# A recurrent attention with an expert layer behind it: y made transposed by products into 32-partition groups, the bonus added on TensorE, four more transposes by DMA

## The chip, the cores and the metric

The kernel runs on one core of a Trainium2 chip. The metric is the device time of one execution in microseconds. Before the change three runs took 178.69 to 178.74 us, with a median of 178.7 us.

## The reference

```python
def _attn_ref(r, k, v, w, u):            # each (4, 8, 768, 48): batch, heads, steps, width
    for t in range(S):
        cur = einsum('bhd,bhe->bhde', u[None] * kt, vt)
        y[:, :, t] = einsum('bhd,bhde->bhe', rt, state + cur)
        state = wt[:, :, :, None] * state + einsum('bhd,bhe->bhde', kt, vt)

def _moe_ref(x, w_in, w_out):            # x (3072, 384), w_in (384, 2048), w_out (2048, 384)
    h = x @ w_in
    g = np.maximum(0.01 * h, h)
    return g @ w_out
...
x = attn_out.transpose(0, 2, 1, 3).reshape(B * S, H * D)
```

Each of 4 x 8 heads keeps a 48 x 48 state that decays per row by w. The output of a step is r times the state, plus the bonus: the sum over d of r k u, times v. The eight heads of a step side by side make a row of 384 numbers, and all 3072 rows go through two dense layers with a leaky rectifier between.

## The kernel before, in words

The steps are cut into 24 chunks of 128. Within a chunk the recurrence is a masked product of r and k, both scaled by running products of w, times v; the state carries what came before. The first four chunks are worked as two pairs (`pair`), whose steps lie interleaved on the partitions; the other 20 are worked one by one (`single`), some of them two at a time in one score step (`run`, `MERGED`). Two of the 20 are the first of their batch and have no state to read.

A single chunk n goes so. SyncE loads w, k, r and v (L708). ScalarE takes the logarithm of w (L718), TensorE sums it over the steps (L724, and totals in L727), VectorE makes the inclusive sum `ci` (L736), ScalarE the two exponentials (L750, L754), VectorE scales r and k into `rk` (L407). r and k are then turned so that the width lies on the partitions (`rkT`): for chunks in `RK_DMA` by one transposing DMA on SyncE's queue (L771), for the others by eight transposes on TensorE (L418) and two copies out of PSUM (L423 on VectorE, L425 on ScalarE). TensorE makes the scores (L864, 48 rows, even and odd heads in the two halves of the array's rows), VectorE masks them into `m` (L795). TensorE adds k times v to the state (L805, L820), and makes y: four products of `rkT` with the decayed state `sb` (L831, 96 columns each) and eight of `m` with `vb`, the bf16 copy of v (L836, 48 columns each). So y has the steps on the partitions.

The bonus runs beside it: GpSimd multiplies k by u and the result by r (L437, L441), VectorE sums it per head (L445), GpSimd multiplies v by that sum into `vs` (L449). For single chunks VectorE adds `vs` to y while it copies y out of PSUM (`add_bonus`, L482). For pairs TensorE adds it by a product with `spread` (L676), and y is copied out after (L686, L688).

The dense layers need y turned, with 384 numbers on 3 x 128 partitions (`xT`). `to_xt` does that by three transposes on TensorE (L468) and a copy out of PSUM (L473 on VectorE, L475 on ScalarE). For the six chunks of `Y_DMA` one transposing DMA does it (L849).

The dense layers take blocks of one or two chunks: up-projections of `xT` with `w_in_b` (L1030), the rectifier on ScalarE (L1045), down-projections (L1060). The last seven blocks use a scheme of seven products for two chunks (`seven`; sums on VectorE in L941, products in L960, output sums in L981).

Everything is issued in an order written out by hand: `ORDER` lists the steps, `FORCE` names the engine of those that have a choice. A small planner inside (`Plan.order`) walks that list, gives out buffers and counts expected times; they only decide how many products of zeros (`warm`, L1099) are put into TensorE's gaps in the first 24 us. [...]

Of the kernel before, what the change touches and what calls it, by code (L numbers as in the profile page):

```python
# [7 lines left out]
F32 = mybir.dt.float32  # L8
BF16 = mybir.dt.bfloat16
AF = mybir.ActivationFunctionType  # L10
ALU = mybir.AluOpType
# [11 lines left out]
class Plan:  # L23
# [75 lines left out]
TY = (0.95, 24, 0.7, -0.6)  # L99
ORDER = [1122, 0, 1, 2, 3, 4, 5, 6, 7, 11, 14, 20, 12, 18, 15, 17, 16, 13, 19, 21, 8, 22, 25, 26, 27, 23, 36,  # L100
# [67 lines left out]
def kernel(  # L168
# [22 lines left out]
    NQ = FF // 512  # L191
    JQ = NJ // NQ

    RK_DMA = {6, 11, 12, 14, 15, 16, 17, 18, 19, 20, 21, 22, 23}
    Y_DMA = {16, 17, 20, 21, 22, 23}
    MERGED = {6, 10, 12, 14, 16, 18, 20}
    LEAD = 4
# [62 lines left out]
    with tc.manual_schedule():  # L260
# [199 lines left out]
        def to_xt(P0, y, yp, s_ye, n):  # L460
            col_of = columns(n)

            def yT():
                return yp.t[:].bitcast(BF16).rearrange("p (g t) -> p g t", t=128)
# [669 lines left out]
```

## Time and profile before

| | us |
|---|---|
| median of three runs | 178.7 |
| profiled execution, its own time | 178.69 |
| its span | 177.0 |
| TensorE busy, products | 170.4 |
| TensorE busy, weight loads | 139.9 |
| VectorE busy | 143.5 |
| ScalarE busy | 114.0 |
| GpSimd busy | 107.3 |

The span runs from the first to the last instruction of the program in the trace. A group line has the code line, the engine, what it writes and reads, the shape and the count; then the busy time, the mean length of one and the idle time of the engine before it with what ended it. In a timeline the first figure is the start, the second the length until the last of the group has ended. Products on TensorE are pipelined and their ends are modelled: the next one starts long before the one before it ends, so lengths overlap, and the cost of a product is read from the difference of two starts.

### The profile page before, as it was taken

The numbers are of one execution on the slowest core, as the hardware profiler recorded it, in microseconds if no ns is written. First come the engines' busy times: TensorE is split into PE (matmuls) and PEld (weight loads), VectorE is DVE, ScalarE is ACT, GpSimd is POOL, SyncE is SP. The second block draws the span as 40 slices with busy tenths as digits, with TensorE's granted clock in tenths as the row PEclk, the third lists the DMA queues.
The fourth block names the chain that finished last, engine by engine and source line by source line (L and its number), as shares of the span: only waits on it lengthen the run. The fifth ranks groups of instructions, "written<-read, shape, count | busy, mean of one in ns | idle before, by whom it ended". The sixth has DMA issues, their size and how long they took to land.

```text
span 177.0 us, 5530 instructions
## 1 busy us (share of the span) xinstructions
PE 170.4 (96%) x2155; PEld 139.9 (79%) x2158; DVE 143.5 (81%) x299; ACT 114.0 (64%) x263; POOL 107.3 (61%) x143
## 2 busy tenths in 40 slices
PE   7999999999999999999999999999999998999993
PEld 2566779867768877777779899899899997799992
DVE  7498935267599899889879999999999999956662
ACT  5676769734677794796379964676769950178500
POOL 5989946486749859879599093391693959100000
PEclk9999999999999999999999999999999999999999
DMA  5999999999999999999999999996999897432104
GB/s 138 261 271 340 350 300 195 351 231 199 201 206 195 191 199 227 163 201 179 198 206 195 197 208 209 163 222 124 210 194 196 188 226 78 118 101 80 44 26 157
DMA packets 115885, 34.25 MB, mean 194 GB/s; under 512 B 108305, under 2 KB 115090, under 8 KB 115858
## 3 DMA queue, kind: packets, MB, share of 16 engines
q1 hardware_dynamic: 115856, 33.89, 93.1%
q8 instruction: 17, 0.28, 0.7%
q14 instruction: 10, 0.08, 0.2%
q10 hardware_dynamic: 2, 0.00, 0.0%
HBM read 25.17 MB, written 4.72 MB: 169 GB/s over the span
## 4 chain that ended last, share of the span: by engine, by line
PE 69%; DVE 15%; ACT 5%; issue 4%; DMA 3%; POOL 2%; DVEq 0%; SPq 0%; ACTq 0%
PE ps L1030 30%; PE ps L1060 13%; PE ps L960 10%; DVE rk L407 3%; DMA rkT<-rk 3%; PE ps L864 3%; DVE in L941 2%; PE ps L418 2%; ACT g L425 2%; PE ps L724 1%; PE ps L836 1%; DVE ci L736 1%; PE ps L518 1%; DVE dg L445 1%; ACT ps L750 1%
## 5 line engine op out<-in xcount | busy, mean ns | idle before, releaser
L1030 PE MATMUL ps<-xT,w_in_b 128*128 128x256 bf16 (+1 forms) x672 | 70.8, 258 | 0.3 <-DVE rk L407 0.2
L1045 ACT ACTIVATE g<-ps 128x512 bf16<-128x512 f32 x96 | 54.4, 598 | 18.1 <-PE ps L1030 16.0
L1030 PEld LDWEIGHTS <-w_in_b 128*128 128x128 bf16 x672 | 56.9, 98 | 7.8 <-issue 0.6
L437 POOL TENSOR_TENSOR ru<-in,ub 128x384 f32<-128x384 f32 x24 | 24.3, 1017 | 13.1 <-DMA in<-in_k_dram 7.0
L1060 PE MATMUL ps<-w_out_b,g 128*128 128x384 bf16 x160 | 31.4, 326 | 0.0
L407 DVE TENSOR_TENSOR rk<-in,ps 128x384 bf16<-128x384 f32 x48 | 24.8, 547 | 6.1 <-ACT ps L754 2.3
L782 POOL TENSOR_TENSOR sb<-s,a 128x384 bf16<-128x384 f32 x18 | 15.6, 875 | 16.6 <-ACT a L745 8.1
L795 DVE TENSOR_TENSOR m<-ps,maskb 128x512 bf16<-128x512 f32 x40 | 25.1, 682 | 0.3 <-PE ps L864 0.2
L441 POOL TENSOR_TENSOR ru<-ru,in 128x384 f32<-128x384 f32 x24 | 23.8, 1000 | 2.1 <-DMA in<-in_r_dram 1.1
L1060 PEld LDWEIGHTS <-g 128*128 128x128 bf16 x160 | 14.1, 97 | 6.8
L449 POOL TENSOR_TENSOR vs<-in,dg 128x384 f32<-128x384 f32 x20 | 17.4, 874 | 3.0 <-DMA in<-in_v_dram 2.1
L960 PEld LDWEIGHTS <-g 128*128 128x128 bf16 x224 | 18.3, 98 | 0.2
L976 ACT COPY o<-ps 128x192 f32<-128x192 f32 x18 | 5.8, 320 | 17.5 <-PE ps L960 15.5
L960 PEld LDWEIGHTS <-in 128*128 128x128 bf16 x168 | 13.6, 98 | 1.9 <-DVE in L941 1.4
L445 DVE TENSOR_REDUCE dg<-ru 128x8 f32<-128x384 f32 x24 | 12.9, 545 | 1.9 <-POOL ru L441 1.7
L457 POOL CAST vb<-in 128x384 bf16<-128x384 f32 x24 | 12.7, 534 | 2.2 <-DMA in<-in_v_dram 2.2
L981 DVE TENSOR_TENSOR o<-ps,o 128x192 f32<-128x192 f32 x35 | 11.6, 351 | 1.9 <-ACT o L976 1.1
L482 DVE TENSOR_TENSOR y<-ps,vs 128x384 bf16<-128x384 f32 x20 | 10.9, 553 | 2.4 <-PE ps L836 2.3
L754 ACT ACTIVATE ps<-ci 128x384 f32<-128x384 f32 x20 | 9.8, 493 | 4.7 <-DVE ci L736 4.1
L718 ACT ACTIVATE lw<-in 128x384 bf16<-128x384 f32 x20 | 9.9, 521 | 4.1 <-DMA in<-in_w_dram 4.1
L736 DVE TENSOR_TENSOR ci<-ps,lw 128x384 f32<-128x384 f32 x20 | 10.9, 551 | 1.8 <-PE ps L724 1.1
L960 PE MATMUL ps<-in,in 128*128 128x192 bf16 x112 | 11.4, 247 | 0.5 <-DVE in L941 0.5
(105 smaller groups left out, 258.8 us busy)
## 6 DMA issues: line engine op xcount, KB each, us to landing
out_dram<-o SPq DMA_DIRECT2D x23, 192.0 KB, 2.8
in<-in_w_dram SPq DMA_DIRECT2D x20, 192.0 KB, 4.7
in<-in_k_dram SPq DMA_DIRECT2D x20, 192.0 KB, 4.2
in<-in_r_dram SPq DMA_DIRECT2D x20, 192.0 KB, 4.2
in<-in_v_dram SPq DMA_DIRECT2D x20, 192.0 KB, 4.1
in<-in_moe_w_out_dram SPq DMA_DIRECT2D x4, 768.0 KB, 6.9
in<-in_moe_w_in_dram SPq DMA_DIRECT2D x2, 768.0 KB, 9.7
in<-in_moe_w_in_dram SPq DMA_DIRECT2D x4, 384.0 KB, 8.1
```

Source lines behind the costliest of these rows:

```text
L407: (nc.gpsimd if e == "POOL" else nc.vector).tensor_tensor(out=o, in0=x, in1=i, op=ALU.mult)
L437: lambda e: nc.gpsimd.tensor_tensor(out=ru.t[:], in0=kv(), in1=ubv, op=ALU.mult),
L441: lambda e: nc.gpsimd.tensor_tensor(out=ru.t[:], in0=ru.t[:], in1=rv(), op=ALU.mult),
L445: lambda e: nc.vector.tensor_reduce(out=dg.t[:], in_=ru.t[:], axis=AX.X, op=ALU.add),
L449: lambda e: nc.gpsimd.tensor_tensor(out=vs.t[:], in0=vv(), in1=dg.t[:].unsqueeze(2).to_broadcast([128, H, D]), op=ALU.mult),
L457: {"POOL": 0.56}, lambda e: nc.gpsimd.tensor_copy(out=vb.t[:], in_=vv()),
L782: lambda e: nc.gpsimd.tensor_tensor(out=sb.t[:].rearrange("p g a d -> p (g a) d"), in0=s_in.t[:].rearrange("p g a d -> p (g a) d"), in1=a_ ...
L795: lambda e, par=par: nc.vector.tensor_tensor(out=m.t[:, par, :, :], in0=sc[par].t[:].rearrange("p (g t) -> p g t", g=NP), in1=maskb[:].uns ...
L960: nc.tensor.matmul(o(), lhsT=x()[:, i, :], rhs=y()[:, i, :], start=fresh, stop=(stop and i == ii[-1]), skip_group_check=True)
L1030: nc.tensor.matmul(hp.t[:, a * N : (a + 1) * N], lhsT=w_in_b[:, t, (j + a) * 128 : (j + a + 1) * 128], rhs=xb.t[:, t, 0:N], start=(a == 0 ...
L1045: lambda e, hp=hp, g=g, j=j, J=J, N=N: nc.scalar.activation(out=g.t[:, j : j + J, 0:N], in_=hp.t[:, 0 : J * N].rearrange("p (a n) -> p a n ...
L1060: nc.tensor.matmul(op.t[:, 0:DM], lhsT=g.t[:, j, off : off + 128], rhs=w_out_b[:, j, :], start=(j == 0), stop=(j == NJ - 1))
```

## The change

y is made turned from the beginning. The operands of its products change places: `vb` and `sb` become the stationary side, cut into pieces of 32 columns, and `m` and `rkT` the moving side, 128 steps wide. Each product so fills 32 partitions of PSUM and 128 columns; `cell` gives the place. Twelve pieces of 32 make the 384 numbers. The eight heads of 48 do not divide by 32, so `vb` gets a layout in which each head has 80 places, the last 32 zero, and the middle piece of each pair of heads is added up from two products. Per single chunk there are 12 products with the state and 16 with v, instead of four and eight.

The bonus is added by TensorE into the same bank: `vs` (now bf16) is the stationary side, the identity matrix the moving one, three products per chunk (for pairs `spread`). Then one copy, on VectorE or ScalarE, takes the bank, now f32, into `xT`. The transposes of y (L468), the addition on VectorE (L482), the copies of the pairs' y (L686, L688) and the DMAs of y (L849) are gone. `RK_DMA` gains chunks 8, 9, 10 and 13. `vb` is cleared once at the start. `ORDER` and `FORCE` are written anew.

```diff
-TY = (0.95, 24, 0.7, -0.6)
...
-    RK_DMA = {6, 11, 12, 14, 15, 16, 17, 18, 19, 20, 21, 22, 23}
-    Y_DMA = {16, 17, 20, 21, 22, 23}
+    RK_DMA = {6, 8, 9, 10, 11, 12, 13, 14, 15, 16, 17, 18, 19, 20, 21, 22, 23}
...
-    make("vb", 6, [128, H, D], BF16)
+    make("vb", 6, [128, NP, 2, 80], BF16)
...
-    make("vs", 4, [128, H, D], F32)
+    make("vs", 4, [128, H, D], BF16)
...
+        for t in pools["vb"]:
+            nc.vector.memset(t[:, :, :, D:80], 0.0)
...
+        def cell(bank, g, i):
+            t, q = divmod(3 * g + i, 4)
+            return bank.t[32 * q : 32 * q + 32, t * 128 : (t + 1) * 128]
+
+        def xt_copy(P0, yp, n, deps):
             col_of = columns(n)
...
             def xcopy(e):
+                src = yp.t[:, 0:DM].rearrange("p (t c) -> p t c", t=KT)
                 if e == "DVE":
-                    nc.vector.tensor_copy(out=col_of(), in_=yT()[:, 0:KT, :])
+                    nc.vector.tensor_copy(out=col_of(), in_=src)
                 else:
-                    nc.scalar.copy(out=col_of(), in_=yT()[:, 0:KT, :])
...
+            return step({"ACT": 0.5, "DVE": 0.55}, xcopy, P0 + 1, deps=deps, reads=[yp], takes=[place[n][0]])
...
+        def turn_y(n, P0, first, m, vb, rkT, sb, vs, deps, s_vs):
+            yp = Buf("ps", "yy")
+
+            def intra(e):
+                for i in range(0 if first else 3):
+                    for p in range(NP):
+                        nc.tensor.matmul(
+                            cell(yp, p, i), lhsT=sb.t[:, p, :, :].rearrange("p a d -> p (a d)")[:, 32 * i : 32 * i + 32],
+                            rhs=rkT.t[:, p, :], start=(i == 0), stop=False, skip_group_check=True)
+                for i, x in ((0, 0), (1, 1), (1, 2), (2, 3)):
+                    for p in range(NP):
+                        nc.tensor.matmul(
+                            cell(yp, p, i), lhsT=vb.t[:, p, :, :].rearrange("p a d -> p (a d)")[:, 32 * x : 32 * x + 32],
+                            rhs=m.t[:, x // 2, p, :], start=(first and x == 0), stop=False, skip_group_check=True)
+
+            s_y = step({"PE": 0.28 if first else 0.44}, intra, P0 + 1, deps=deps,
+                reads=[m, vb, rkT] + ([] if first else [sb]), takes=[yp])
+
+            def add_vs(e):
+                for t in range(KT):
                     nc.tensor.matmul(
+                        yp.t[:, t * 128 : (t + 1) * 128],
+                        lhsT=vs.t[:].rearrange("p h d -> p (h d)")[:, t * 128 : (t + 1) * 128], rhs=ident[:],
+                        start=False, stop=True, skip_group_check=True)
+
+            s_yb = step({"PE": 0.18}, add_vs, P0 + 1, deps=[s_y, s_vs], reads=[yp, vs])
+            xt_steps[n] = [xt_copy(P0, yp, n, [s_yb])]
...
-            s_ye = add_bonus(P0, y, yp, vs, s_y, s_vs)
-            if n not in Y_DMA:
-                xt_steps[n] = [to_xt(P0, y, yp, s_ye, n)]
-            else:
...
+            turn_y(n, P0, first, m, vb, rkT, sb, vs, [*s_m, *s_T, s_vb, s_sb], s_vs)
```

The pairs' products change in the same way: their products with v use 64 rows and 32 columns of the array, two row halves for two output banks, 64 of them per pair instead of 32, and 12 products with the state instead of four.

More of the change, by code (lines that the diff above doesn't have):

```diff
@@ L673, in add_vs @@
                 for j in range(2):
-                    for x in range(2):
-                        q = slice(64 * x, 64 * x + 64)
-                        nc.tensor.matmul(
-                            yps[x].t[:, 0:DM], lhsT=spread[q, j, :], rhs=vss[j].t[q, :, :].rearrange("p h d -> p (h d)"),
-                            start=False, stop=(j == 1), skip_group_check=True)
-            s_yb = step({"PE": 0.4}, add_vs, P0 + 1, deps=[s_y, *s_vss], reads=[*yps, *vss])
-            for x in range(2):
-                y = Buf("y")
-                def evac_y(e, y=y, x=x):
-                    if e == "DVE":
-                        nc.vector.tensor_copy(out=y.t[:], in_=heads(yps[x].t))
-                    else:
-                        nc.scalar.copy(out=y.t[:], in_=heads(yps[x].t))
-                s_ye = step(
-                    {"ACT": 0.48, "DVE": 0.55}, evac_y, P0 + 1, deps=[s_yb] + [s_yi] * x, reads=[yps[x]], takes=[y])
-                xt_steps[n + x] = [to_xt(P0, y, yps[x], s_ye, n + x)]
-                rows[n + x] = out[b * S + x * L : b * S + (x + 1) * L, :]
+                    for t in range(KT):
+                        for x in range(2):
+                            q = slice(64 * x, 64 * x + 64)
+                            nc.tensor.matmul(
+                                yps[x].t[:, t * 128 : (t + 1) * 128],
+                                lhsT=vss[j].t[q, :, :].rearrange("p h d -> p (h d)")[:, t * 128 : (t + 1) * 128],
+                                rhs=spread[q, j, :], start=False, stop=(j == 1), skip_group_check=True)
@@ L805, in sums @@
                         nc.tensor.matmul(
[L806 removed]
+                            pp.t[:, p * 2 * D : (p + 1) * 2 * D].rearrange("p (a d) -> p a d", a=2),
                             lhsT=rk.t[:, 1, 2 * p : 2 * p + 2, :].rearrange("p h d -> p (h d)"),
[L808 removed]
+                            rhs=vb.t[:, p, :, 0:D],
                             start=True, stop=True, skip_group_check=True)
```

102 lines of the change are left out of this document (38 added, 64 removed), and 104 rows, old and new, of the table ORDER.

## The prediction

> **What bounds the kernel now.** I read the page first, then the stretches, then TensorE's own timeline.
>
> ```profile
> span 177.0 us, 5530 instructions
> PE 170.4 (96%) x2155; PEld 139.9 (79%) x2158; DVE 143.5 (81%) x299; ACT 114.0 (64%) x263; POOL 107.3 (61%) x143
> ...
> PEclk9999999999999999999999999999999999999999
> ...
> PE 69%; DVE 15%; ACT 5%; issue 4%; DMA 3%; POOL 2%; DVEq 0%; SPq 0%; ACTq 0%
> ```
>
> TensorE is busy 96% of the span at a full clock and holds 69% of the chain that ended last. Its busy time is modelled, so the starts have to show whether it is really full.
>
> ```profile
> 54.13 0.81 PE L1060 MATMUL ps<-w_out_b,g 128*128 128x384 bf16 x4
> 54.78 0.83 PE L1030 MATMUL ps<-xT,w_in_b 128*128 128x128 bf16 x12
> 55.45 0.33 PE L831 MATMUL ps<-sb,rkT 128*128 128x96 bf16 x4
> 55.62 0.36 PE L836 MATMUL ps<-vb,m 128*128 128x48 bf16 x8
> 55.82 0.83 PE L1030 MATMUL ps<-xT,w_in_b 128*128 128x128 bf16 x12
> ...
> 56.86 0.32 PE L724 MATMUL ps<-lw,trev 128*128 128x384 bf16 x1
> 57.02 0.24 PE L727 MATMUL ps<-ones,lw 128*128 128x1 bf16 x4
> ```
>
> Columns: start, length, then the group. Differences of starts give the rates: 0.65 us for 4 products of 384 columns, 0.67/12 = 0.0558 for one of 128 columns, 0.17 for the four state products, 0.20 for eight of 48 columns (0.0255 each, more than 48 columns would need). No gap stands between groups, so from here on each added column is paid for. The gaps that do exist:
>
> ```profile
> 48.35 0.81 PE L1060 MATMUL ps<-w_out_b,g 128*128 128x384 bf16 x4
> 49.20 0.49 PE L836 MATMUL ps<-vb,m 128*128 128x48 bf16 x8
> 49.81 0.40 PE L418 MATMUL ps<-ident,rk 128*128 128x128 bf16 x4
> ```
>
> ```profile
> 149.01 0.83 PE L960 MATMUL ps<-w_out_b,in 128*128 128x192 bf16 x8
> 150.38 0.84 PE L960 MATMUL ps<-in,in 128*128 128x192 bf16 x8 [0.53 <-DVE in L941]
> 151.61 0.83 PE L960 MATMUL ps<-w_out_b,in 128*128 128x192 bf16 x8 [0.40 <-DVE in L941]
> 152.38 0.40 PE L864 MATMUL ps<-rkT 48*128 48x128 bf16 x8
> ```
>
> At 48 to 50 us, 0.85 + 0.61 pass where 0.65 + 0.20 are work: 0.6 lost. At 149 to 152, 1.37 and 1.23 pass for eight products each, which take 0.66 elsewhere (118.40, in the chain further down): 1.3 lost to late sums of VectorE. That is 1.9 us in all, the most that a relief of VectorE can return after the start.
>
> ```profile
> 127.00:152.00 25.00, 24.04 (x316) 21.86 (x315) 24.79 (x46) 14.36 (x39) 19.00 (x23) 1.00 0.99 179
> ```
>
> Columns: stretch, length, busy time of TensorE, its weight loads, VectorE, ScalarE, GpSimd, then clock, DMA share, GB/s. In the stretch of the second loss VectorE is full (24.79 of 25.00).
>
> **The change, part by part.** TensorE first, chunks 4 to 23. Removed: 18 sets of state and value products at 0.17 + 0.20 and two sets of 0.20, 7.06 us; the transposes of y of 14 chunks, 42 products of 128 columns at 0.0558, 2.34; the transposes of r and k of four chunks, 32 products, 1.79.
>
> Added: 12 products per chunk with state (18) and 16 for each of 20, 536 in all, each 128 columns wide into 32 partitions, four partition groups side by side. Do four run at once? The trace has no such form; the nearest is the pairs' score product, 48 rows into 64 partitions, two row halves by two column halves:
>
> ```profile
> 11.08 0.64 PE L632 MATMUL ps<-g 48*64 48x128 bf16 x32 [0.17 <-ACT g L425]
> ```
>
> ```profile
> L632 PE MATMUL ps<-g x64: 213/216/241, 11.1 to 19.0; 48*64 48x128 bf16 x64
> ```
>
> One of these lasts 216 ns (the middle figure), so 32 starts lie within 0.42: 0.0137 each, a quarter of 0.0558. Four parts of the array did run at once, with weight loads between them. I take 0.0140 per product, 536 x 0.0140 = 7.50. The bounds are 0.0137 and, if nothing runs at once, 0.0558 (+22 us). The bonus adds 60 products of 128 columns, 3.35.
>
> Each change of the array's division has a price too. The scores of the chunks use two row halves:
>
> ```profile
> 35.60 0.33 PE L724 MATMUL ps<-lw,trev 128*128 128x384 bf16 x1
> 35.85 0.40 PE L864 MATMUL ps<-rkT 48*128 48x128 bf16 x8
> 36.18 2.77 PE L1060 MATMUL ps<-w_out_b,g 128*128 128x384 bf16 x16
> ```
>
> ```profile
> 52.24 0.62 PE L864 MATMUL ps<-rkT 48*128 48x128 bf16 x16
> 52.80 0.82 PE L1060 MATMUL ps<-w_out_b,g 128*128 128x384 bf16 x4
> ```
>
> Eight take 0.33 to the next start, sixteen 0.56: 0.23 per eight, so 0.10 is the way out. The product of 384 columns before them holds 0.25 where 0.16 is usual (56.86 to 57.02): 0.09 for the way in. That is 0.20 for a visit. In the changed order the 20 chunks' new products stand in 15 runs, each with whole-array products on both sides; the scores keep 13 visits. Whether a division by columns costs what one by rows costs, no row shows; bounds are 0 and 0.20, and I take 0.20, since the score row is the only one: 3.0 us.
>
> Sum: 7.50 + 3.35 + 3.0 - 7.06 - 2.34 - 1.79 = +2.7 us of TensorE.
>
> VectorE and ScalarE:
>
> ```profile
> L482 DVE TENSOR_TENSOR y<-ps,vs 128x384 bf16<-128x384 f32 x20 | 10.9, 553 | 2.4 <-PE ps L836 2.3
> ...
> L473 DVE COPY xT<-ps 128x384 bf16<-128x384 bf16 x9 | 3.1, 355 | 1.5 <-PE ps L468 1.5
> ...
> L1071 DVE COPY o<-ps 128x384 f32<-128x384 f32 x5 | 2.8, 550 | 0.0
> ```
>
> ```profile
> L475 ACT COPY xT<-ps 128x384 bf16<-128x384 bf16 x9 | 4.1, 481 | 3.1 <-PE ps L468 3.0
> ...
> L1073 ACT COPY o<-ps 128x384 f32<-128x384 f32 x5 | 2.4, 477 | 0.2 <-PE ps L1060 0.2
> ```
>
> VectorE loses 20 additions (11.1) and nine copies (3.2) and gets five copies of the new, wider form, priced as the other f32 copy, 0.55 (2.75); ScalarE has 19 of them at 0.48 instead of nine at 0.48. That is 11.5 us less on VectorE, before other copies that the new order hands to it; the exact size does not enter the sum, only whether it is late. Off TensorE's path this is worth nothing; where it was late it can return 0 to 1.9. I take 1.3, the loss at 149 to 152, because the additions of the chunks then in work leave VectorE; the earlier 0.6 stays.
>
> Queues: six transposing DMAs of y go, four of r and k come.
>
> ```profile
> 93.88 1.24 SPq L771 DMA_TRANSPOSE rkT<-rk  x1
> ...
> 117.50 2.48 SPq L849 DMA_TRANSPOSE xT<-y  x2
> ```
>
> Both kinds hold SyncE's queue for 1.24, so loads behind them get 2.5 us more room in all; the four new ones (chunks 8, 9, 10 and 13) stand early, among the loads of later chunks, which queue behind them while they wait for r and k. I cost it at nothing: the whole-array products of other chunks run meanwhile. Without that cover, one landing of 5.12 us (below) would be bare. GpSimd's narrower product and padded cast stay on an engine that is 61% busy, at nothing, bounded by a tenth of a microsecond per chunk either way. A new wait: the bonus product waits on TensorE for GpSimd's product, and everything on TensorE queues behind it.
>
> The start:
>
> ```profile
> 2.59 0.70 DVE rk L270 x5
> ...
> 3.56 0.56 DVE o L384
> ...
> 4.84 0.50 PE ps L395
> ...
> 18.53 0.74 ACT w_in_b L344
> 19.32 2.14 PE ps L1030 x18
> ...
> 108.18 5.12 DMA rkT<-rk
> ...
> 118.40 0.66 PE ps L960 x8
> ```
>
> In this chain of waits five clearings take 0.70; six more, of the padding of v, come ahead of the first addition: +0.85. Later the chain passes a weight cast that need not move. On the other hand only 6 up-projections, not 18, now precede the second pair's products (256 columns each, so twice 0.0558: 12 x 0.11 = 1.3 more afterwards). Against that, the pairs' y is no longer copied, transposed and copied. Bounds 0 and +2.2; I take +0.4.
>
> Sum: 2.7 - 1.3 + 0.4 = +1.8. The profiled execution took 178.69 us (span 177.0 and 1.7 around it), the median of the runs is 178.7, so 178.69 + 1.8 = 180.5 us.
>
> **Rivals.** First, the weight loads do not hide. In the new form all tiles lie in the same rows, and every product is preceded by a load; in the score row half the neighbours differ in rows. If each product then costs what the 48-column ones cost, 0.0255, 536 x 0.0115 = +6.2: 186.7. Against it: in the whole array, loads in the same rows already pass under products (128 columns each 0.0558). [...]
>
> Second, the other side: entering a division by columns costs nothing, because all rows stay in use. Then the 3.0 falls away at the 15 visits: 177.5, faster. It decides once a visit costs less than 0.08 (1.8/15 below 0.20). For it: the price is shown for row halves alone. Against it: the output products after the scores need nothing from them and still start late, so the price belongs to the change of division.
>
> Third, the stalls do not go but move: TensorE waits for the bonus or for a landing of r and k. The 1.3 is not gained and 20 waits of 0.1 come: 183.8. For it: the 5.12 landing in the chain; against it: GpSimd is idle 39% of the span.
>
> Fourth, the terms cancel: a visit at half the price and a little more relief, within 0.2% (0.36 us, about what a measurement of this kernel can tell from no change).
>
> **How the numbers follow.** Forecast 0.43, its own range 179.1 to 182.2; first rival 0.10; second 0.27; third 0.13; fourth 0.07. Faster: the second and a tail of the forecast, 0.28; same 0.08; slower 0.64. The range reaches to the second rival with all 1.9 returned, 176.9, and between the third and the first, 185.0.
>
> **What would show it.** Starts of the new products 0.014 apart in runs of 28 confirm the rate; 0.025 or more brings the first rival. The whole-array group ahead of them 0.1 late and the one behind 0.1 late confirm the visit. Gaps of TensorE gone at 149 to 152 confirm the relief; gaps ahead of the bonus products speak for the third rival. The first long run of up-projections after the second pair should begin within 1 us of 23.3; much earlier or later, and the start was mis-sized. A total of TensorE starts that falls instead of rising makes the forecast wrong.

## The result, and the profile after

The changed kernel takes 183.05 us (median of 4 runs, 182.72 to 183.49), the kernel before 178.72 us beside it: a ratio of 1.0243, 95% interval 1.0216 to 1.0271. It is slower by 4.3 us, where 1.8 was forecast. The profiled execution took 183.34 us, its span is 181.6 us (177.0 before).

From the page of the changed kernel:

```profile
span 181.6 us, 6248 instructions
...
PE 175.3 (97%) x2549; PEld 141.3 (78%) x2552; DVE 137.3 (76%) x284; ACT 114.3 (63%) x259; POOL 106.1 (58%) x142
...
q8 instruction: 20, 0.33, 0.8%
...
PE 88%; DVE 5%; DMA 3%; SPq 1%; issue 1%; DVEq 0%
```

TensorE's share of the chain rose from 69% to 88%. The third line is a queue that the prediction never looked at. Its 20 packets (0.33 MB, 16,384 bytes each in the trace) stand beside the 2549 products and 2552 loads of the line above, 255 to a packet; in the kernel before 17 packets stand beside 2155 and 2158, 254 to a packet. By this count I take it for the queue that brings TensorE's instructions.

First the part after the start. TensorE's timeline of the changed kernel (start, length, group):

```profile
45.13 1.46 PE L1048 MATMUL ps<-w_out_b,g 128*128 128x384 bf16 x8
46.52 0.41 PE L689 MATMUL ps<-m,vb 128*32 128x128 bf16 x16
46.86 1.48 PE L1048 MATMUL ps<-w_out_b,g 128*128 128x384 bf16 x8
```

```profile
59.41 0.35 PE L684 MATMUL ps<-rkT,sb 128*32 128x128 bf16 x12
59.58 0.40 PE L689 MATMUL ps<-m,vb 128*32 128x128 bf16 x16
59.81 0.34 PE L684 MATMUL ps<-rkT,sb 128*32 128x128 bf16 x12
59.97 0.40 PE L689 MATMUL ps<-m,vb 128*32 128x128 bf16 x16
60.30 0.82 PE L1048 MATMUL ps<-w_out_b,g 128*128 128x384 bf16 x4
```

Twelve products of 32 columns pass in 0.17 us and sixteen in 0.23: 0.014 each, a quarter of the 0.0558 of a product of 128 columns in the whole array, so four do run at once, and their loads, 95 and 97 ns each on average, are hidden. The visit is there too: eight products of 384 columns before the group take 1.39 where 8 x 0.162 = 1.30 is usual (0.09 in), and sixteen new ones hold 0.34 to the next start instead of 0.22 (0.12 out): 0.21 in all.

```profile
119.89 0.83 PE L948 MATMUL ps<-w_out_b,in 128*128 128x192 bf16 x8
120.56 0.82 PE L948 MATMUL ps<-in,in 128*128 128x192 bf16 x8
121.22 0.82 PE L948 MATMUL ps<-in,g 128*128 128x192 bf16 x8
121.88 0.82 PE L1018 MATMUL ps<-xT,w_in_b 128*128 128x256 bf16 x6
```

The products that waited for VectorE's late sums now follow each other every 0.66. After 28 us the starts show two waits in the whole span, 0.6 us together, at 44.87 and 139.72. The kernel before has 2.5 us by the same count: the prediction's two places come to 1.7, and it passed over 0.3 at 44.31, 0.2 at 113.35 and 0.2 at 145.98.

Now the start, where the rest went:

```profile
13.89 0.64 PE L619 MATMUL ps<-g 48*64 48x128 bf16 x32
...
20.44 0.92 PE L1087 MATMUL ps<-zeros 128*128 128x512 bf16 x5
21.30 0.64 PE L619 MATMUL ps<-g 48*64 48x128 bf16 x32
21.87 0.83 PE L1018 MATMUL ps<-xT,w_in_b 128*128 128x256 bf16 x6
22.53 1.19 PE L1087 MATMUL ps<-zeros 128*128 128x512 bf16 x7
...
24.37 0.91 PE L645 MATMUL ps<-m,vb 64*32 64x128 bf16 x64
...
26.45 0.71 PE L1018 MATMUL ps<-xT,w_in_b 128*128 128x256 bf16 x5
```

The same in the kernel before:

```profile
18.59 0.64 PE L632 MATMUL ps<-g 48*64 48x128 bf16 x32
19.32 2.14 PE L1030 MATMUL ps<-xT,w_in_b 128*128 128x256 bf16 x18
...
21.74 0.56 PE L657 MATMUL ps<-vb,m 64*128 64x48 bf16 x32
...
23.25 2.14 PE L1030 MATMUL ps<-xT,w_in_b 128*128 128x256 bf16 x18
```

The first pair's scores stand at 13.89 (11.08 before), the second's at 21.30 (18.59), its products of y at 24.37 (21.74), and the gapless work begins at 26.45 (23.25) with only 6 up-projections done, not 18. So 2.8 us are lost ahead of the first scores and come back nowhere. Products of zeros stand where work stood. For these kernels I count, in the first 30 us, the time that dummy products hold TensorE (start of each to the next start). Beside it stands how far TensorE is behind the kernel before at 30 us: the products that both have in common and that are still to be done, each at its usual spacing:

```
kernel                                dummy   behind at 30 us (us)
before                                  8.5    0
changed                                12.3    3.8
x1  clearings later                    11.2    3.6
x3  start in the old order              8.7    3.5
x5  few dummy products                  5.5    5.2
x9  all in the old order               10.2    2.4
x10 x9, clearings later                 9.6    1.9
x13 x10, dummy products halved          9.9    2.7
x16 x10, pairs in the old form          8.9   -0.5
x17 before, pairs in the new form       9.5    0.8
x11 before, new order of the start     13.4    5.0
x12 changed, with extra visits         12.4    4.1
```

The start costs 3.8 us: 29 up-projections of 256 columns (3.2), three of 128 (0.2) and four products of 384 columns (0.65) are left that the kernel before has done by then, against one product of 384 columns done ahead of it (0.16). What the pairs save by their new form is already in it. One profiled execution places such milestones only to within some half a microsecond: x12 below has the changed kernel's start unchanged, and its first scores stand at 13.36.

### The profile page after: what moved, and what is told of

Same layout as the page of the kernel before. It is cut to its first block, busy times and chain, and to the rows that moved or that the text cites. A ratio compares the mean times of both kernels' runs of the same rounds, so it can differ in the third digit from the quotient of the medians.

```text
span 181.6 us, 6248 instructions
## 1 busy us (share of the span) xinstructions
PE 175.3 (97%) x2549; PEld 141.3 (78%) x2552; DVE 137.3 (76%) x284; ACT 114.3 (63%) x259; POOL 106.1 (58%) x142
## 4 chain that ended last, share of the span: by engine, by line
PE 88%; DVE 5%; DMA 3%; SPq 1%; issue 1%; DVEq 0%
PE ps L1018 33%; PE ps L948 16%; PE ps L1048 15%; PE ps L1087 4%; PE ps L852 3%; DMA in<-in_r_dram 3%; PE ps L689 2%; PE ps L684 2%; PE ps L698 2%; PE ps L416 2%; PE ps L736 2%; PE ps L505 2%; PE ps L817 2%; DVE rk L405 1%; SPq L720 1%
## 5 line engine op out<-in xcount | busy, mean ns | idle before, releaser
L1033 ACT ACTIVATE g<-ps 128x512 bf16<-128x512 f32 x96 | 55.0, 601 | 17.7 <-PE ps L1018 15.9
L435 POOL TENSOR_TENSOR ru<-in,ub 128x384 f32<-128x384 f32 x24 | 23.8, 1000 | 12.9 <-DMA in<-in_k_dram 10.2
L1048 PE MATMUL ps<-w_out_b,g 128*128 128x384 bf16 x160 | 30.7, 326 | 0.0
L447 POOL TENSOR_TENSOR vs<-in,dg 128x384 bf16<-128x384 f32 x20 | 17.6, 880 | 7.5 <-DMA in<-in_v_dram 4.5
L455 POOL CAST vb<-in 128x384 bf16<-128x384 f32 x24 | 11.9, 502 | 5.9 <-DMA in<-in_v_dram 4.6
L471 ACT CAST xT<-ps 128x384 bf16<-128x384 f32 x19 | 8.7, 480 | 9.6 <-PE ps L698 7.9
L1087 PE MATMUL ps<-zeros 128*128 128x512 bf16 (+1 forms) x52 | 12.4, 367 | 1.4 <-DVE zeros L257 1.3
L762 ACT ACTIVATE ps<-ps 128x384 f32<-128x384 f32 x20 | 9.4, 472 | 6.2 <-DVE ci L748 6.1
L948 PE MATMUL ps<-in,g 128*128 128x192 bf16 x112 | 11.5, 246 | 0.0
```

Source lines behind the costliest of these rows:

```text
L435: lambda e: nc.gpsimd.tensor_tensor(out=ru.t[:], in0=kv(), in1=ubv, op=ALU.mult),
L447: lambda e: nc.gpsimd.tensor_tensor(out=vs.t[:], in0=vv(), in1=dg.t[:].unsqueeze(2).to_broadcast([128, H, D]), op=ALU.mult),
L948: nc.tensor.matmul(o(), lhsT=x()[:, i, :], rhs=y()[:, i, :], start=fresh, stop=(stop and i == ii[-1]), skip_group_check=True)
L1033: lambda e, hp=hp, g=g, j=j, J=J, N=N: nc.scalar.activation(out=g.t[:, j : j + J, 0:N], in_=hp.t[:, 0 : J * N].rearrange("p (a n) -> p a n ...
L1048: nc.tensor.matmul(op.t[:, 0:DM], lhsT=g.t[:, j, off : off + 128], rhs=w_out_b[:, j, :], start=(j == 0), stop=(j == NJ - 1))
L1087: nc.tensor.matmul(warm.t[:, 0:n], lhsT=zeros[:, 0:128], rhs=zeros[:, 0:n], start=True, stop=True, skip_group_check=True)
```

## The experiments

Times are compared by their ratio to the kernel before on the same chip, whose median was 178.7 us at the result and 179.0 to 179.95 in the batches below; "span" is that of the profiled execution.

**First batch: is it the clearings, or the order?**

x1 moves the six clearings behind the copy of u:

```diff
-        for t in pools["vb"]:
-            nc.vector.memset(t[:, :, :, D:80], 0.0)
...
                 nc.scalar.copy(out=ub[:], in_=u_ps.t[:, 0:DM])
+            for t in pools["vb"]:
+                nc.vector.memset(t[:, :, :, D:80], 0.0)
```

> The changed kernel, with the six clearings of v's padding moved behind VectorE's copy of u's row, where VectorE stood idle for 2.1 us. Theory S (the loss is in the start: TensorE has no gaps later, so each microsecond by which the pairs' work is late arrives at the end): 183.05 - 0.85 = 182.2. Rival T (the loss is in the steady part: visits, waits, slow products) and rival W (the start waits for the weights, so the clearings are hidden): 183.0.

Measured: 185.52 us, ratio 1.0313 (1.025 to 1.0376), span 182.8. The first scores did come 1.85 us sooner (12.04), and the second pair's products 1.63 (22.74), and yet nothing was won. Its TensorE timeline:

```profile
22.74 0.59 PE L645 MATMUL ps<-m,vb 64*32 64x128 bf16 x42
24.78 0.35 PE L645 MATMUL ps<-m,vb 64*32 64x128 bf16 x22 [1.45 <-issue]
...
26.29 0.38 PE L1018 MATMUL ps<-xT,w_in_b 128*128 128x256 bf16 x2
```

In brackets stands the idle time and what ended it: 1.45 us in the middle of one step, between products whose operands were all there, "issue", so nothing that the profile shows.

x2 gives the first pair's sums their old order:

```diff
-14, 20, 15, 17, 16, 12, 18, 19, 13, 21,
+14, 20, 12, 18, 15, 17, 16, 13, 19, 21,
```

> The changed kernel, with the first pair's sums, totals and exponentials in the order of the kernel before (the sums for the first exponentials ahead of the eight totals). In the changed kernel the second group of sums starts at 8.33 us, 1.7 after the first; before, 0.6 after it. Theory S: between 0.3 and 1.1 us faster, 182.0 to 182.75. Rivals T and W: 183.0.

Measured: 184.15 us, ratio 1.0241 (1.0184 to 1.0299), span 182.0, no difference from the changed kernel's 1.0243. First scores 0.5 us sooner, no more than x12 shows without any change to the start; then 0.78 us of the same wait in the same step.

x3 issues the first 136 steps in the old order and on the old engines, with x1's later clearings.

> The changed kernel, with the first 136 steps (both pairs, the first weights and up-projections) in the order and on the engines of the kernel before, the clearings later as in x1, the rest in the changed order. Theory S: the second pair's products end near 23.2 us again instead of 26.4, so 183.05 - 2.9 = 180.2, and what is left over 178.7 is the steady part (+2.8 of TensorE, -1.4 of stalls). Rival T: over 182.5. Rival W: about 182, as the weights then set the time.

Measured: 185.96 us, ratio 1.0303 (1.0225 to 1.0381), span 182.6. First scores at 10.83; 0.67 us of the odd wait at 17.55, among transposes of r and k; second pair's products at 22.47, and again 1.21 us of idleness in the middle of them; then 1.5 us for the fifth chunk's w, which this mixed order fetches late.

x4 puts six clearings of the same size into the kernel before:

```diff
         nc.vector.memset(ones[:], 1.0)
+        for x in range(6):
+            nc.vector.memset(pads[x][:, :, :, 0:32], 0.0)
```

> The kernel before, with six clearings of the same size put on VectorE at the same place; nothing else is changed. Theory S: 178.7 + 0.85 = 179.55. Rival W (the delay is absorbed by the waits for weights and casts before the first up-projections): 178.7 to 178.9.

Measured: ratio 1.0032 (0.9988 to 1.0076), no difference that can be told. The product of u came 0.84 late (5.68), the first scores at 10.89 (11.08 before). So in the old order the clearings are absorbed. In the changed order they are not: there the first scores moved by 1.85 (x1).

In x1, x2 and x3 the odd wait ended at 24.78, 25.25 and 24.29, and it stood each time before TensorE's record number 702 (weight loads, products and the few records of its sequencer, counted from 0). That suggested the instruction queue.

**Second batch: dummy products, and instructions.**

x5 lets the dummy products end early in the changed kernel; x6 does so in x1, x8 in x3:

```diff
-    WARM_UNTIL = 24.0
+    WARM_UNTIL = 8.0
```

> The changed kernel, the TensorE's dummy products that fill planned gaps only where the plan puts them before 8 us (24 us before); nothing else differs. Theory C (the dummy products hold the pairs' work up: between 5 and 26.6 us they are 27.7% of the changed kernel's chain of waits and 7.2% of the old one's): the first pair's scores (L619) come before 13.3 us (13.89), the second's before 20.3 us (21.30), and the time is 181.0 to 182.0 us. Theory F (a page of 256 TensorE instructions arrives only at about 24.8 us, the page beginning at TensorE instruction 702): the same milestones may move, but the dense work after the second pair starts no earlier than about 25.3 us (26.45), since fewer dummy products also put that page's edge later in the pair's work; time 181.5 to 182.3 us. Theory T (the dummy products stand only in waits that exist anyway): milestones within 0.3 us of the changed kernel's, TensorE idle in their place, time 182.9 to 183.2 us; slower than that if the granted clock falls.

Measured: 186.83 us, ratio 1.0373 (1.0314 to 1.0431), span 184.8. First scores at 12.09, second at 20.95:

```profile
20.95 0.87 PE L619 MATMUL ps<-g 48*64 48x128 bf16 x32 [0.69 <-ACT g L423]
...
24.02 0.74 PE L645 MATMUL ps<-m,vb 64*32 64x128 bf16 x64 [0.65 <-DVE m L631]
...
27.30 0.40 PE L668 MATMUL ps<-spread,y 64*128 64x128 bf16 x8 [1.53 <-issue]
```

So the dummy products had held up the first scores (1.8 us, or 1.3 against x12) but hardly the second pair's work (0.35 us), which now waits for ScalarE and VectorE. The odd wait came here as well, later, and in another step. And the granted clock fell: 0.982 over the span (0.999 in the changed kernel), the 32 score products lasting 0.87 where they take 0.64 in the changed kernel. If all of the fall lies in the first 30 us, it is 0.89 there, an estimate from 184.8 x 0.018 / 30. Leaving the dummy products out is no gain.

> x1 (the six clearings of v's padding behind the copy of u) with the dummy products planned after 8 us left out. Theory F: x1's wait of 1.45 us at TensorE instruction 702 moves to a later product or shrinks below 0.6 us, because some 35 dummy products (70 instructions) fewer stand ahead of it; with C the dense work starts by 25.3 us; time 180.8 to 182.0 us. Theory T: as x1, 185.5 us, with the 1.45 us wait still in the middle of the second pair's products.

Measured: 185.36 us, ratio 1.0281 (1.0226 to 1.0335), span 182.5, clock 0.981. The 1.45 us wait of x1 shrank to 0.2, as forecast, and the first scores stand at 11.64; the dense work began at 25.93, not by 25.3, and the time did not follow.

> x3 (the first 136 steps in the old order and on the old engines, clearings later) without the dummy products planned after 8 us. Theories C and F: x3's wait of 1.21 us at instruction 702 falls below 0.5 us or goes, the dense work starts by 24.8 us; time 180.3 to 182 us, the less the wait for the fifth chunk's w (1.5 us at 27.3 us in x3) takes its place. Theory T: 185.5 to 186 us as x3.

Measured: 186.01 us, ratio 1.0343 (1.0298 to 1.0389), span 184.6, clock 0.991. x3's wait inside the second pair's products is gone; 0.58 us of the odd wait stand inside the second pair's scores instead, and waits for VectorE and ScalarE ahead of the scores (2.1 us) and for w (1.8 us) took over.

x7 cuts the dummy products of the kernel before into four:

```diff
-nc.tensor.matmul(warm.t[:, 0:n], lhsT=zeros[:, 0:128], rhs=zeros[:, 0:n], ...)
+for q in range(0, n, n // 4):
+    nc.tensor.matmul(warm.t[:, q:q + n // 4], lhsT=zeros[:, 0:128], rhs=zeros[:, 0:n // 4], ...)
```

> The kernel before, each 512-column dummy product of the start as four of 128 columns and each 128-column one as four of 32: the same columns, some 100 products (200 TensorE instructions) more ahead of the dense work. Theory F: TensorE now waits with nothing shown at its instructions 446 and 702, the first until about 17.7 us, the second until about 24.8 us (fetches start at 15.2 and 22.3 us and took 2.5 us until use in x1); the old kernel's dense work, 23.3 us, then starts at 24.8 us or later; time 179.8 to 181.5 us. If TensorE's instructions never make it wait: no such gap, 178.7 to 179.2 us.

Measured: 181.07 us, ratio 1.0068 (1.0028 to 1.0109), span 178.1. No wait at either place, dense work from 23.34 as before: the expectation fell. The records of the instruction queue say why. I had taken the packets to start at fixed times (15.2 and 22.3 us in the kernel before); with more instructions executed early they also started early (11.0 and 17.2 us).

**Third batch: order or products?**

x9 has the changed arithmetic, but every step in the old order and on the old engines from end to end (each bonus where the transposes of y were, the six copies that replace DMAs of y shortly behind their bonus; r and k of chunks 8, 9, 10 and 13 transposed on TensorE again). x10 is x9 with x1's later clearings.

> All of the changed kernel's arithmetic (new products, bonus on TensorE, clearings at the start) with the old order of all steps on the old engines from end to end, each bonus in the place of the old transposes; r and k of chunks 8, 9, 10 and 13 stay on TensorE as before. Theory O (the late start, some 2.9 us, comes from the order and the engines laid out anew, not from the new products): first scores (L619) by 11.6 us (13.89 in the changed kernel), second by 19.5 (21.30), dense work from 24 to 25 us; span 178.5 to 180.8 us, time 180.0 to 182.3 us, the upper end if a page of TensorE instructions is late again (some 1.2 us). Theory P (the new products and clearings themselves make the start late): first scores after 13 us, time 183 us or more.

> x9 with the six clearings behind the copy of u. Theory O with x4 (clearings are absorbed in the old order): within 0.4 us of x9. Theory S (the clearings stand ahead of the first pair): 0.5 to 0.9 us below x9, the u product at 4.8 us in place of 5.7.

Measured: x9 185.85 us, ratio 1.0355 (1.0308 to 1.0402), span 184.1; x10 185.27 us, ratio 1.0329 (1.0274 to 1.0384), span 183.5. TensorE of x10:

```profile
16.35 0.39 PE L418 MATMUL ps<-ident,rk 128*128 128x128 bf16 x4
17.55 0.62 PE L418 MATMUL ps<-ident,rk 128*128 128x128 bf16 x8 [0.81 <-issue]
...
22.58 0.59 PE L647 MATMUL ps<-m,vb 64*32 64x128 bf16 x46
24.29 0.34 PE L647 MATMUL ps<-m,vb 64*32 64x128 bf16 x18 [1.12 <-issue]
...
25.44 1.27 PE L1020 MATMUL ps<-xT,w_in_b 128*128 128x256 bf16 x10
```

The first scores are on time (10.69) and the second nearly (19.22), so with the old order the chain through ScalarE and VectorE is as before; but two odd waits, 0.8 + 1.1 us (0.9 + 1.4 in x9), delay the dense work to 25.44. The old order alone does not mend the start. Theory O's milestones came; its dense work and its time did not. The clearings are worth 0.6 us here by spans and medians, though the intervals of x9 and x10 overlap.

Most of x10's time is lost elsewhere. Of the 6.5 us of span that it has over the kernel before, 1.9 are the start (the table), and 5.0 are more work of TensorE after 30 us where the changed kernel has 2.3: the transposes of r and k of four chunks stay on it (1.8), and the new products stand in 19 runs, not 15, at 0.21 a visit (0.8). Waits after 30 us, 0.5 shorter, and the end, 0.3 longer, are the rest.

x11 is the other way round: the old arithmetic, with the first steps in the changed kernel's order.

> The kernel before, its first steps (to about 27 us) in the changed kernel's order and on its engines, the transposes of y directly ahead of what needs them; no new products. Theory O: first scores (L632) at 12.5 us or later (11.08 before), second at 20 us or later (18.59), dense work from 25 us or later (23.25), time 180.5 to 182 us. Theory P: milestones within 0.5 us of the old kernel's, time 178.7 to 179.5 us.

Measured: 185.55 us, ratio 1.036 (1.0301 to 1.0419), span 183.5.

```profile
20.15 2.43 PE L1100 MATMUL ps<-zeros 128*128 128x512 bf16 x12
22.93 0.81 PE L1031 MATMUL ps<-xT,w_in_b 128*128 128x256 bf16 x6 [0.35 <-DVE xT L474]
...
24.19 0.56 PE L658 MATMUL ps<-vb,m 64*128 64x48 bf16 x32
...
26.05 0.82 PE L1031 MATMUL ps<-xT,w_in_b 128*128 128x256 bf16 x6
```

The milestones moved less than expected (first scores 11.96, second 19.23, so 0.9 and 0.6 late), but the second pair's products come at 24.19 and the dense work at 26.05 with 6 up-projections done, as in the changed kernel. It is not the same delay. VectorE makes the second pair's masks at 19.77, 0.7 later than before, and then this:

```profile
22.17 0.61 DVE L474 COPY xT<-ps 128x384 bf16<-128x384 bf16 x2
```

The up-projections at 22.93 wait for this copy of the first pair's y, and the second pair's products stand in TensorE's queue behind them. The changed kernel makes its xT of the first pair on ScalarE at 18.87, and its loss is complete at the first scores. So x11 shows 0.6 to 0.9 us of lateness that the new order brings with the old arithmetic; the other 1.8 at the products come of the old arithmetic in a new order, and say nothing of the changed kernel. (The rest of x11's time is lost where the two orders meet.)

x12 puts one product of zeros, added to the bank, between the two groups of 18 chunks:

```diff
+                if not first:
+                    nc.tensor.matmul(
+                        yp.t[:, 0:128], lhsT=zeros[:, 0:128], rhs=zeros[:, 0:128], start=False, stop=False,
+                        skip_group_check=True)
                 for i, x in ((0, 0), (1, 1), (1, 2), (2, 3)):
```

> The changed kernel with one ordinary product of 128 columns (zeros, added to the bank) between the products of the state and those of v in each of the 18 chunks that have both, so that TensorE leaves the 32-column groups and comes back once more in each. At the 0.23 us that the trace gives for one visit, and 0.06 us for the product: 18 x 0.29 = 5.2 us more, less where TensorE would have waited: 187 to 188.5 us. If a visit cost nothing (rival 2): 18 x 0.06 = 1.1 us more, 184.1 us.

Measured: 188.35 us, ratio 1.05 (1.0453 to 1.0548), span 186.5, 4.9 more than the changed kernel's.

```profile
59.70 0.35 PE L684 MATMUL ps<-rkT,sb 128*32 128x128 bf16 x12
59.98 0.23 PE L688 MATMUL ps<-zeros 128*128 128x128 bf16 x1
60.14 0.41 PE L693 MATMUL ps<-m,vb 128*32 128x128 bf16 x16
60.38 0.34 PE L684 MATMUL ps<-rkT,sb 128*32 128x128 bf16 x12
```

From the first group's last start to the second's first start 0.311 us pass, 0.046 without the extra product: 0.265 more, of which 0.056 is the product. A visit costs 0.21, alike in all 18 places; 18 x 0.265 = 4.8 of the 4.9.

x12 shows one thing more, since its start is the changed kernel's own, line by line:

```profile
24.03 0.59 PE L645 MATMUL ps<-m,vb 64*32 64x128 bf16 x42
25.24 0.35 PE L645 MATMUL ps<-m,vb 64*32 64x128 bf16 x22 [0.63 <-issue]
```

In this execution the second pair's products began 0.34 us sooner than in the changed kernel's (24.37), and then stood in their middle until 25.24. The odd wait belongs to the changed start too.

**Fourth batch: are the odd waits the instruction stream?**

x13 is x10 with each dummy product cut in two halves: the same columns, 80 more instructions.

> x10 with each dummy product of the start split in two halves (512 columns as two of 256, 128 as two of 64): the same columns, some 40 products (80 TensorE instructions) more. Theory F2 (TensorE takes its instructions in pages of 256; in the loaded first 28 us a page comes 5 to 7.6 us after the edge of the one before was crossed; x10 crosses its edges at 12, 17.5 and, for want of the page, 24.3 us): the edges fall some 60 to 80 instructions earlier in the work, about 11, 15.2 and 22.5 us, so the wait of 1.1 us inside the second pair's products shrinks below 0.4 us or goes, though instructions were added; the first of the two (0.8 us) may stay, at an earlier instruction. Dense work from 24.2 to 25.0 us (25.44), time 184.0 to 184.9 us (185.27). Rival R (the waits belong to those products, by operands or ports, not to the instruction stream): both waits at the same products as in x10, 185.3 us.

Measured: 185.97 us, ratio 1.0324 (1.0272 to 1.0377), span 185.0.

```profile
15.71 0.28 PE L670 MATMUL ps<-spread,y 64*128 64x128 bf16 x3
17.86 0.45 PE L670 MATMUL ps<-spread,y 64*128 64x128 bf16 x9 [1.87 <-issue]
...
24.34 0.97 PE L647 MATMUL ps<-m,vb 64*32 64x128 bf16 x64
```

At the pair's products of y next to nothing is left of the wait, and the one that stood among transposes of r and k stands among bonus products. By number, nothing moved. From the records of TensorE and of the instruction queue (us; the packet is the one that I take to bring the instructions from the edge on):

```
run   edge at record   previous edge crossed   packet starts   edge crossed   idle   held
x1    702              17.49                   22.32           24.78          1.45   1.67
x3    447              12.18                   15.05           17.55          0.67   0.89
x3    702              17.55                   21.42           24.29          1.21   1.44
x10   449              12.04                   15.06           17.54          0.80   1.02
x10   705              17.54                   21.46           24.29          1.11   1.33
x12   705              18.77                   22.39           25.24          0.63   0.84
x13   449              11.20                   15.21           17.85          1.86   2.08
x13   705              17.85                   21.97           24.60          0.01   0.23
x17   449              11.66                   14.74           17.30          0.94   1.16
x17   705              17.30                   20.73           23.23          0.30   0.52
changed  702           19.12                   22.21           24.93          none   0.18
before   702           19.01                   22.28           27.38          none   0.00
changed  2494          79.85                   80.36           88.84          none   -
```

The idle time runs from the modelled end of what came before; "held" runs from the record before the edge to the first one behind it, 0.00 to 0.05 where nothing waits within a step. The edges lie 256 records apart (a few records are missing, hence 447 or 449, 702 or 705), whatever product stands there, and in every row that was held the first record behind the edge comes 2.5 to 2.9 us after the packet's start. I read this as TensorE waiting for its instructions. In the rows of the start the packet begins 2.9 to 4.8 us after the edge before it was crossed, in the last row 0.5 us after. From edge to edge 5.4 to 7.3 us pass in the eleven rows that were held; in the kernel before it is 8.4, and nothing was held. The changed kernel itself stood 0.18 us at its edge, 2.7 us after its packet's start: it came there just when the packet did. The dense work takes longer for 256 records (9.0 us in the last row). The pairs' new products do not: 64 of them and their 64 loads pass in 0.68 us (17.49 to 18.17 in the changed kernel). The shift did not pay in x13, because the first wait grew by what the second lost (expected was below 0.4 for the second, which came, and dense work from 24.2 and a time below 185, which did not: 26.14 and 185.97).

x14 gives x10 the four transposes by DMA, x15 is x14 with x13's halves.

> x10 with r and k of chunks 8, 9, 10 and 13 transposed by DMA as in the changed kernel, each DMA in the place of the chunk's last transpose, and xT of chunks 22 and 23 copied on VectorE. By the prediction's own term for the four chunks (1.79 us of TensorE removed) and x10's last wait (0.9 us for xT on ScalarE) gone: span 180.8 to 181.8 us (183.5), time 182.4 to 183.6 us. Rival: the DMAs land late for the scores (waits at L852 for rkT, as 0.9 us in x5): 184 to 185 us.

> x14 with the dummy products split as in x13: x13's gain on x10 again if theory F2 holds, 0.3 to 1.3 us below x14 and so 181.3 to 183.0 us; under rival R the same as x14.

Measured: 190.93 us, ratio 1.0601 (1.0548 to 1.0654), and 189.67 us, ratio 1.0531 (1.0483 to 1.0579). Misses, by the rival that x14 names and more. TensorE's waits in x14:

```profile
PE ps L852 <- DMA rkT<-rk: 3.6, 1, 3.6
```

In the old order one such DMA lands 3.6 us late. The changed kernel has no wait for rkT of that kind, so the four DMAs are free in its order. The waits at the edges in x14 (0.84 and 0.84) and x15 (1.89, none) repeat those of x10 and x13. x15 came 1.3 us below x14, as it expected at most, but not by these waits, whose sums are alike.

**Fifth batch: the pairs alone.** x16 is x10 with the pairs in the old form; x17 is the kernel before with only the pairs in the new form.

> x10 with the two pairs in the old form (y by products of the masked scores, copied out, transposed): only the single chunks have the new products; old order throughout. Theory G (the pairs' new products run through TensorE's instruction pages too fast for the loaded start): no wait over 0.2 us at instructions 449 and 705, dense work after the second pair from 23.0 to 23.7 us (25.44 in x10, 23.24 before); span 181.0 to 181.8 us (183.5 less 2.2), time 182.4 to 183.4 us. Rival (the start is late for other reasons): dense work after 24.5 us, time 184.5 to 185.5 us as x10.

> The kernel before with only the two pairs in the new form (v padded and cleared behind the copy of u), all single chunks and the order as before (two buffers in place of four for y). Theory G: waits of 0.6 to 1.2 us with nothing shown at instructions 449 and 705, dense work from 25.0 to 25.7 us (23.24), span 178.8 to 179.6 us (177.0), ratio to the kernel before 1.010 to 1.015. Rival (the pairs cost only their products, some 0.3 us): dense work by 23.8 us, ratio below 1.004.

Measured: x16 184.39 us, ratio 1.0293 (1.0251 to 1.0334), span 183.1.

```profile
20.95 0.58 PE L667 MATMUL ps<-vb,m 64*128 64x48 bf16 x32
...
22.50 2.14 PE L1044 MATMUL ps<-xT,w_in_b 128*128 128x256 bf16 x18
...
41.59 0.32 PE L762 MATMUL ps<-lw,trev 128*128 128x384 bf16 x1 [1.66 <-ACT lw L756]
```

The start is whole again: no wait at an edge, dense work at 22.50 (25.44 in x10), and TensorE 0.5 us ahead of the kernel before at 30 us. That speaks for theory G. The total followed only in part: at 41.59 TensorE waits 1.66 us for a w whose DMA ScalarE had itself waited 4.03 us for. The same place has 1.39 in x4 and 0.60 in x17, so the wait is not of the new products. The 6.1 us of span over the kernel before are -0.5 at the start, +1.3 of waits after 30 us (3.8 for 2.5), +0.3 behind the last product, and the same +5.0 of TensorE's work as in x10.

Measured: x17 179.78 us, ratio 1.0032 (1.0008 to 1.0055), span 177.6, below the range given.

```profile
17.31 0.62 PE L420 MATMUL ps<-ident,rk 128*128 128x128 bf16 x8 [0.94 <-issue]
...
23.23 0.34 PE L676 MATMUL ps<-m,vb 64*32 64x128 bf16 x18 [0.30 <-issue]
...
24.39 3.30 PE L1045 MATMUL ps<-xT,w_in_b 128*128 128x256 bf16 x33
```

Both waits are there, the second shorter, and the dense work is 1.14 late (24.39), but only 0.8 us of work is behind at 30 us, since the pairs' y needs no transposes afterwards. So the pairs' new form costs about 0.6 us here, not 2. The ratios of x10 and x16 (1.0329 and 1.0293) put it at about 0.6 as well, with intervals that overlap, though the two are 2.4 apart at 30 us.

No version tried beats the kernel before.

## Why the prediction was wrong

**The sign was right and the measured time lies in the outer range, 176.9 to 185.0, though not in the forecast's own; the start was mis-sized, and that is most of the miss.** The step that failed is "Bounds 0 and +2.2; I take +0.4". Measured +3.8, far above its upper bound. The term counted six clearings and a moved row of up-projections, and took most of it as hidden because the chain later passes a weight cast that need not move. The runs showed two things in its place.

First, nothing was hidden. The first pair's scores were 2.8 late and the second's 2.7. Moving the clearings takes 1.85 off the first scores in the changed order (x1) and 0.45 where the dummy products after 8 us are left out too (x5 to x6); in the old order next to nothing (x4, and 0.2 from x9 to x10). So a delay of 0.84 at the product of u grew to 1.85 in the new order with its dummy products. The other 0.96 is about what the new order brings with the old arithmetic, 0.6 to 0.9 (x11). I had compared what stands before the scores, not when it can run.

Second, the instructions. The starts of x1, x2 and x3 brought the second pair's new products sooner, stood idle within them at the edge of an instruction packet (1.45, 0.78 and 1.21 us) and gave the gain back; so did x12 with the changed kernel's own start (0.63). x9 and x10 pay 2.3 and 1.9 us there, x16 with the old pairs pays nothing. The prediction counted TensorE's columns and never its instructions. In the changed kernel's profiled execution the two coincide: the second pair comes so late that the edge holds it only 0.18 us. Mending the first alone gained nothing (x1). No run has the new pairs, an early start and full clock without a wait at the edge, so how the two share the 3.8 us stays open.

**Steady TensorE, +2.7: near, by parts that were off.** The rates held: 536 x 0.014 = 7.5, bonus 3.35, 15 visits at 0.21 = 3.15 (3.0 forecast). But what was removed had held TensorE for 11.7 us in the kernel before, its waits left out, not 11.2: the transposes of y 2.6 and the products of y 7.3, since short groups among others cost more than the rates of long runs (0.062 a transpose instead of 0.0558). From 30 us to the last product TensorE has 147.9 us, 143.7 before; without the 3.8 left over from the start, and with the waits below taken off both, it is 2.3 more.

**Relief of VectorE, -1.3: the mechanism right, the size too small.** Waits after 28 us went from 2.5 to 0.6: -1.9. The stall at 149 to 152 went, as said. "1.9 in all, the most that a relief of VectorE can return" had missed three places with 0.8; the earlier one, which was to stay, went as well. x9 and x10 have no stall for these sums either, so that part belongs to the arithmetic; but in the old order 1.5 us of new waits for xT came in its place.

**A term that was not there.** From the start of the last product to the end of the span 3.2 us pass in the kernel before and 3.7 in the changed one, +0.5. No run shows why.

**Sum.** 2.3 - 1.9 + 3.8 + 0.5 = 4.7, the difference of the spans.

**Rivals.** The first, loads that do not hide, is refuted by 0.014 per product. Here all tiles lie in the same rows, and their loads of 95 and 97 ns are hidden all the same. The second, free visits, is refuted by x12: 0.21 each by columns, where the prediction read 0.20 by rows. The third gives 183.8, nearest to the measured 183.05, by luck: its new waits for bonus or landings did not come in the changed kernel; x14 shows that the landing it named is real in another order. The fourth had no part.

**What was to show it.** The named sign, up-projections within 1 us of 23.3, did its work: 26.45 said at once that the start was mis-sized.

## What to carry to other kernels

Count a change's instructions, not only its columns: the small products here, 0.014 us each instead of 0.0558, also used up instructions about four times as fast as products of 128 columns in the whole array, and in the first 28 us, where TensorE was held, 5.4 to 7.3 us lay between two edges 256 records apart. Read a new order's start by when the other engines deliver, milestone by milestone, not by what was moved. Putting the old order back is a separate experiment from taking the new arithmetic out. A mixture of the two has delays of its own (x11, x14), so follow its delay to the step where it arises before charging it to either side.

## What the runs showed of the hardware

Products of 128 rows by 32 columns, 128 columns moving, ran four at once at 0.014 us each in the changed kernel (twelve in 0.17 us, sixteen in 0.23; 0.0558 for one of 128 columns in the whole array), with their loads, 95 and 97 ns on average, hidden. Leaving the whole array for them and coming back cost 0.21 us (x12).

The instruction queue moved packets of 16,384 bytes, 20 beside 5101 records of TensorE in the changed kernel. The waits that I read as waits for instructions stood at edges 256 records apart. The longest was 1.9 us, in the first 28 us (x13); after 30 us the changed kernel and the one before have no wait at any edge. Why the packet began 2.9 to 4.8 us after the edge before it in the start, and 0.5 us after it at 80.36, no run shows: DMA moved 274 GB/s in the changed kernel's first 30 us and 190 between 60 and 120, with a busy share of 1.09 and 1.03.

Without dummy products after 8 us the granted clock was 0.982 over the span in x5, 0.981 in x6 and 0.991 in x8, against 0.999 in the changed kernel. TensorE's listed waits over the span come to 9.9, 7.1 and 8.9 us in them, and to 2.5 in the changed kernel. No run shows what lowers the clock.
